# Attention and two MLPs on one core: the planner's order replaced by written tables, with filler products in PE's early waits

## The chip, the cores and the metric

The kernel runs on one core of a Trainium2 chip. The metric is the device time of one execution in microseconds (us). The core has TensorE (PE, with its weight loads as PEld), VectorE (DVE), ScalarE (ACT), GpSimd (POOL), and SyncE (SP), which issues nearly all DMAs.

## The reference

Three stages follow one another on 4 sequences of 576 positions: block-causal attention (8 heads of 64, blocks of 64 positions), an MLP with a gate from a three-tap convolution over positions, and an MLP whose second half is normalized and mixed over positions. All is float32.

```python
scores = scale * np.matmul(q, k.transpose(0, 1, 3, 2))
scores = np.where(block_i >= block_j, scores, -1000000000.0)
attn = np.exp(scores - np.max(scores, axis=-1, keepdims=True))
attn = attn / (np.sum(attn, axis=-1, keepdims=True) + 1e-09)
x = heads_side_by_side(np.matmul(attn, v))          # [4, 576, 512]
...
h = np.maximum(x @ w_in, 0.0)                       # moe: 512 -> 1024
x = (h / (1.0 + np.exp(-conv3(h, conv_w)))) @ w_out # 1024 -> 512
...
u, v = halves(np.maximum(x @ w2_in, 0.0))           # moe2: 2 x 512
v_n = (v - mean(v)) / np.sqrt(var(v) + 1e-06)
gated = u * (np.einsum('ts,bsd->btd', w_spatial, v_n) + b_spatial[None, :, None])
out = gated @ w2_out
```

## The kernel before, in words

Most products are made of three: each float32 operand is split into a rounded high part and the rest, and PE multiplies high by high, high by rest and rest by high. The splits are work for ACT (high part), DVE and POOL (the rest).

PE's work is cut into 429 steps of five streams, and each stream keeps its own order. The attention goes through 16 pairs of heads, p = 0 to 15.

- **x** (80 steps, five for each pair, x5p to x5p+4): four products `max_step` (L566) whose row maxima DVE reduces, and one transpose `max_tr` (L643) of the maxima. x4 is the transpose of pair 0, x9 that of pair 1, x24 that of pair 4. Between the fourth and the fifth stands DVE's `max_up`. After the transpose ACT or DVE copies the result to `mt`, and a DMA spreads it as a row of `mq`; x3, x5, x10 and so on may take both banks of the ring `mo` in place of one of `st`.
- **s** (66 steps, `score`, L731): scores of a pair, for which the row of maxima must have come; ACT takes the exponential and so frees the slot. For pair 0, s0 and s1 are the first part, without the row, and s2 and s3 add the row to the same slots.
- **v** (16 steps, `av`, L753): probabilities by values; `v_out` and `s_out` copy the result and the sums out, and `norm_a` (L825) sends the sums through three DMAs and multiplies.
- **m** (129 steps, `in1` L857 and `out1` L900): the first MLP. `out1` stores its result to DRAM through a buffer `y`.
- **p** (138 steps, L1135 to L1298): the second MLP, after the attention is over; it begins in the last steps of m.

Around PE run tasks: `prep_pair` (L496) loads a pair's keys and queries and makes kp and qp (its tasks `one` and `ends`; for pairs that are not multiplied in plain float32 it also subtracts the rest), `split64` (L446) loads and splits 64K weights, `load_vs` loads values, `add_up` adds exponentials, `combine` and `store` finish the output.

The order of everything is made when the program is built. Class `Order` (L104) keeps a clock with a cost for each step and task (functions `t_act`, `t_dve` and so on) and at each moment gives each engine the ready task of the best priority, in `kick` (L185), and PE a step, by `pick_at` (L1001), which weighs how far the m stream lags behind the attention against constants such as `AHEAD` and `TILE_ON`. Buffer slots are given out first free, first taken (`grab`, L224). The engines then run their instructions in the order of that emission; each waits on semaphores for what it needs.

PSUM has the ring `st` (three slots of two banks) and `mo` (two banks). Sixteen products of 256 columns on a set tile (`spin`, L1037) run on PE before the first data are there; they write to the last slot of `st`. SP issues, in order: pair 0's two parts, `ident`, the first `v`, `cwr`, pairs 1 and 2, then weights.

Of the kernel before, what the change touches and what calls it, by code (L numbers as in the profile page):

```python
# [16 lines left out]
NP = H // 2  # L17
# [12 lines left out]
AHEAD = (0.05, 2.01, -0.09, 0.71)  # L30
# [30 lines left out]
EARLY_M = 3  # L61
TILE_ON = 0.55
JOIN = 0.3
S_FIRST = 3
HOLD = 0
STKEEP = 2
MARGIN = 0
STICK = 0
# [11 lines left out]
XE = (0.95, 13.95)  # L80
XMO = 11
XK = 0.35
WR = 2
SPIN = 16
SLACK = 0.8
# [17 lines left out]

class Order:  # L104
# [9 lines left out]
    def __init__(self, rings):  # L114
        self.t = 0.0
        self.heap = []
        self.seq = 0
        self.done = set()
        self.waiting = {}
        self.free = dict(rings)  # L120
# [5 lines left out]
        self.flying = 0  # L126
        self.pick = None
        self.cost = 0.0
        self.tile = False
        self.port = 0.0  # L130
        self.when = {}
        self.extra = {}
        self.times = {r: [-9.0] * n for r, n in rings.items()}
        self.slots = {r: [None] * n for r, n in rings.items()}
# [5 lines left out]
    def spawn(self, gen, group="x", lag=0.0):  # L140
        self.live[group] = self.live.get(group, 0) + 1
        self.push(self.t + lag, lambda: self.advance(gen, group))

    def advance(self, gen, group, got=None):
        while True:
# [11 lines left out]
            elif kind == "take":  # L157
                n = it[2] if len(it) > 2 else 1
                if self.free[it[1]] >= n and not any(r[0] == it[1] for r in self.ring_wait):
                    got = self.grab(it[1], n)  # L160
# [15 lines left out]
    def enqueue(self, it, gen, group):  # L176
        eng, dur, fn = it[:3]
        lat = (it[3] if len(it) > 3 else 0.0) + (0.03 if eng == "ACT" else 0.0)
        prio = it[4] if len(it) > 4 else 1
        port = it[5] if len(it) > 5 else False  # L180
        self.seq += 1
        heapq.heappush(self.ready.setdefault(eng, []), (prio, self.seq, dur, fn, lat, gen, group, port))
# [20 lines left out]
    def mark(self, key):  # L203
        self.done.add(key)
        self.when[key] = self.t
# [3 lines left out]
    def release(self, ring, slots):  # L209
        self.free[ring] += len(slots)  # L210
        self.times[ring] += [self.t] * len(slots)
        self.slots[ring] += slots
        for r in list(self.ring_wait):
            if r[0] == ring:
                if self.free[ring] < r[1]:
                    break
                got = self.grab(ring, r[1])
                self.ring_wait.remove(r)
                self.push(self.t, lambda r=r, got=got: self.advance(r[2], r[3], got[0] if r[1] == 1 else got))
# [4 lines left out]
    def grab(self, ring, n):  # L224
        self.free[ring] -= n
        del self.times[ring][:n]
        got = self.slots[ring][:n]
        del self.slots[ring][:n]
        return got

    def reset(self, ring, slots):
        self.free[ring] = len(slots)
        self.times[ring] = [self.t] * len(slots)
        self.slots[ring] = list(slots)

    def can(self, step, margin=0.0):
        if "alts" in step:
            for ring, keep in step["alts"]:
                step["ring"], step["rings"] = ring, step["base"] + [(ring, 1)]
                if self.free[ring] > keep + self.extra.get(ring, 0) and self.fits(step, margin):  # L240
                    return True
            return False
        return self.fits(step, margin)

    def fits(self, step, margin):
        return all(k in self.done and self.when[k] <= self.t - margin for k in step["needs"]) and all(
            self.free[r] >= n and self.times[r][n - 1] <= self.t - margin
            for r, n in step["rings"])

    def pe(self):  # L250
# [5 lines left out]
        got = {r: self.grab(r, n) for r, n in step["rings"]}  # L256
# [7 lines left out]
        def end():  # L264
# [5 lines left out]
            for gen, group in after or ():  # L270
                self.spawn(gen, group, self.PE_HOP)
# [13 lines left out]
def dma(size, fn, prio=0, issue=0.48):  # L285
    yield ("SP", issue, fn, 0, prio)
    yield ("sleep", 0.5)
# [21 lines left out]
def attn_moe_moe2_kernel(  # L309
# [104 lines left out]
    ALTS = [("mo", 0), ("st", 0)]  # L414

    mk = att.tile([128, S], F32R, name="mk")
# [29 lines left out]
    def split64(src, hi, lo, key, prio=None):  # L446
        prio = P_W if prio is None else prio
        unit = {"w1i": 0, "w1o": 8, "w2i": 16, "w2o": 24}[key[0]] + key[-1] + (4 * key[1] if len(key) > 2 else 0)
        yield ("take", "wr")
        home = "wn" if key[0] != "w2i" and (od.free["wn"] or od.free["x1"] <= X1KEEP[key[0] == "w1o"]) else "x1"  # L450
# [4 lines left out]
        yield from dma(524288, lambda: nc.sync.dma_start(  # L455
# [4 lines left out]
        yield ("free", "wr")  # L460
# [20 lines left out]
    def load_pairs():  # L481
        for p in range(NPAIR):
            if not f32_scores(p):
                yield ("take", "late")
# [3 lines left out]
            od.spawn(prep_pair(p, RAW[p], slot), "att")  # L488
# [3 lines left out]
    def first_load(o, i, part):  # L492
        yield from dma(o.shape[1] * o.shape[2] * 512, lambda: nc.sync.dma_start(out=o, in_=i), -1)
        yield ("mark", ("raw", 0, part))

    def prep_pair(p, t, slot):  # L496
# [4 lines left out]
        if p:  # L501
            yield from dma(2 * S * 4 * 128, lambda: nc.sync.dma_start(out=t, in_=src), P_RAW)
# [19 lines left out]
        for i, c in enumerate(parts):  # L522
# [3 lines left out]
            od.spawn(one(act(kp[:, c], t[:, 0, c], n), ("kpq", p, i, 0)), "att")  # L526
            od.spawn(one(second(qp[:, c], t[:, 1, c], n), ("kpq", p, i, 1)), "att")
# [6 lines left out]
        od.spawn(ends(), "att")  # L534
# [11 lines left out]
        yield ("free", "late")  # L546
# [3 lines left out]
    def load_vs():  # L550
        yield ("sleep", 0.06)
        for p in range(NPAIR):
# [3 lines left out]
            yield from dma(327680, lambda: nc.sync.dma_start(out=t, in_=vt[b, g]), P_V)  # L556
# [968 lines left out]
```

## Time and profile before

| | us |
|---|---|
| median of 3 runs | 614.19 (613.38 to 614.73) |
| profiled execution | 615.53 |
| its span, first to last instruction | 613.8 |
| PE busy | 582.1 (95%) |
| DVE busy | 458.7 (75%) |
| ACT busy | 252.8 (41%) |
| POOL busy | 220.3 (36%) |

The profiled execution's time is the span and 1.7 us around it. PE's matmuls are pipelined and their ends are modelled. The granted clock is the share of 2.4 GHz that PE was given; it has two levels, 1.2 and 2.4 GHz. Idle time of an engine counts only where it holds up the engine that sets the end. A line such as L342 is that of a helper (`mm`) through which most products go.

### The profile page before, as it was taken

The page shows a single profiled execution, that of the slowest core. Times are in us where ns is not written, and L with a number is a line of the kernel's source. Part 1 is how long each engine was busy: PE and PEld are TensorE (multiplying, and loading weights), DVE is VectorE, ACT ScalarE, POOL GpSimd, SP SyncE. Part 2 cuts the span into 40 slices and gives each one's busy share as a digit, 9 for nine tenths or more (in the row PEclk, how much of TensorE's full clock was granted, in tenths as well). Part 3 has the DMA queues.
Part 4 walks back from the last instruction along what each step waited for, and adds up shares of the span by engine and source line. Part 5 has one row for each costly group of instructions (what it writes and reads, how often), then busy time and mean ns, then how long its engine had stood idle before and what let it go on. Part 6 is the DMA issues. An engine that isn't in the chain of part 4 may idle for free.

```text
span 613.8 us, 11943 instructions
## 1 busy us (share of the span) xinstructions
PE 582.1 (95%) x4596; PEld 519.1 (85%) x4596; DVE 458.7 (75%) x930; ACT 252.8 (41%) x517; POOL 220.3 (36%) x269
## 2 busy tenths in 40 slices
PE   6888879989999999999999999999999999999997
PEld 4556657969897788779988998999989999998996
DVE  4898899986929986985936399986697576368256
ACT  3465555644345632435626174636153023013101
POOL 5321343565352647435525253642212112022020
PEclk7698989999999999999999999999999999999999
DMA  7364543024031233212020374434713300610002
GB/s 238 109 206 150 183 160 141 1 90 129 30 129 42 67 115 120 81 60 82 1 78 21 105 250 132 153 105 116 237 36 106 127 19 1 194 40 2 28 31 79
DMA packets 43543, 61.23 MB, mean 100 GB/s; under 512 B 8949, under 2 KB 34293, under 8 KB 43486
## 3 DMA queue, kind: packets, MB, share of 16 engines
q1 hardware_dynamic: 43226, 60.37, 30.3%
q8 instruction: 36, 0.59, 0.4%
q14 instruction: 21, 0.17, 0.1%
q0 software_dynamic: 256, 0.09, 0.1%
q10 hardware_dynamic: 4, 0.00, 0.0%
HBM read 46.08 MB, written 14.23 MB: 98 GB/s over the span
## 4 chain that ended last, share of the span: by engine, by line
PE 56%; DVE 27%; DMA 5%; ACT 4%; issue 3%; POOL 2%; SPq 1%; ACTq 0%; DVEq 0%; POOLq 0%
PE mo L342 33%; PE s L342 9%; DVE cc L882 5%; PE st L350 4%; PE st L712 4%; DVE cc L886 3%; DVE mx L592 3%; PE st L704 2%; DMA w_raw<-in_w2o_dram 2%; DMA raw<-in_kq_dram 2%; PE st L716 2%; DVE g L356 2%; DVE w_f L443 2%; PE st L587 1%; DVE w_raw L441 1%
## 5 line engine op out<-in xcount | busy, mean ns | idle before, releaser
L342 PE MATMUL mo<-x,w1i_h 128*128 128x290 f32 x504 | 109.1, 303 | 1.7 <-DVE y L919 1.2
L342 PE MATMUL mo<-g,w1o_h 128*128 128x288 f32 x464 | 98.3, 298 | 0.8 <-ACT h L876 0.4
L882 DVE SCALAR_TENSOR_TENSOR cc<-h,cwt,cc 128x288 f32<-128x288 f32 x128 | 77.8, 623 | 18.1 <-ACT cc L879 17.5
L342 PEld LDWEIGHTS mo<-x,w1i_h 128*128 128x128 f32 x504 | 83.5, 189 | 5.7 <-issue 2.3
L342 PEld LDWEIGHTS mo<-g,w1o_h 128*128 128x128 f32 x464 | 76.2, 189 | 3.2 <-issue 1.5
L342 PE MATMUL mo<-x,w1i_l 128*128 128x290 f32 x252 | 75.3, 299 | 0.0
L342 PE MATMUL mo<-g,w1o_l 128*128 128x288 f32 x232 | 68.5, 295 | 0.0
L353 POOL TENSOR_SCALAR g<-cc 128x288 fp32r<-128x288 f32 x64 | 40.1, 632 | 77.7 <-DVE cc L886 69.7
L725 ACT ACTIVATE e<-st 128x640 f32<-128x640 f32 (+1 forms) x64 | 52.5, 836 | 31.1 <-PE st L716 30.4
L353 POOL TENSOR_SCALAR g<-ga 128x288 fp32r<-128x288 f32 x40 | 19.0, 474 | 108.3 <-DVE ga L1225 73.4
L342 PE MATMUL mo<-x,w2i_h 128*128 128x288 f32 x256 | 52.4, 296 | 0.5 <-ACT u L1199 0.3
L342 PEld LDWEIGHTS mo<-x,w1i_l 128*128 128x128 f32 x252 | 47.8, 190 | 0.0
L350 PE MATMUL st<-e,v 128*64 128x448 f32 (+4 forms) x384 | 47.2, 395 | 0.4 <-ACT e L725 0.3
L592 DVE TENSOR_REDUCE mx<-st 128x2 f32<-128x128 f32 (+3 forms) x64 | 42.3, 684 | 4.9 <-PE st L587 3.4
L350 PEld LDWEIGHTS st<-e,v 128*64 128x64 f32 x384 | 25.3, 138 | 23.2 <-issue 17.0
L342 PEld LDWEIGHTS mo<-g,w1o_l 128*128 128x128 f32 x232 | 43.6, 188 | 0.1
L342 PEld LDWEIGHTS mo<-x,w2i_h 128*128 128x128 f32 x256 | 41.4, 188 | 1.5 <-ACT u L1199 1.2
L716 PE MATMUL st<-mq,mk 64*128 64x320 f32 (+1 forms) x192 | 39.4, 406 | 1.2 <-DMA mq<-mt 1.2
L879 ACT ACTIVATE cc<-h,cwt 128x288 f32<-128x288 f32 x64 | 34.3, 536 | 12.9 <-DVE g L356 6.9
L342 PE MATMUL s<-w2i_h,x 128*128 128x512 f32 x128 | 39.5, 390 | 0.0
L342 PE MATMUL mo<-ws_h,vnh 128*128 128x288 f32 x135 | 39.4, 296 | 0.0
L884 ACT ACTIVATE cc<-cc 128x288 f32<-128x288 f32 x64 | 28.1, 440 | 27.1 <-DVE cc L882 26.6
(184 smaller groups left out, 1432.1 us busy)
## 6 DMA issues: line engine op xcount, KB each, us to landing
x2d<-y SPq DMA_DIRECT2D x32, 288.0 KB
x<-x2d SPq DMA_DIRECT2D x16, 576.0 KB
raw<-in_kq_dram SPq DMA_DIRECT2D x15, 576.0 KB
v<-in_vt_dram SPq DMA_DIRECT2D x16, 320.0 KB
rb<-rd SPq DMA_DIRECT2D x32, 144.0 KB
out_dram<-o SPq DMA_DIRECT2D x32, 144.0 KB
x<-in_w2i_dram SPq DMA_DIRECT2D x8, 512.0 KB
w_raw<-in_w1i_dram SPq DMA_DIRECT2D x4, 512.0 KB
```

Of the source, the lines that this page charges most:

```text
L342: nc.tensor.matmul(o, w, x, start=start, stop=stop)
L350: nc.tensor.matmul(o[row:row + m], w, x, start=start, stop=stop)
L353: nc.gpsimd.tensor_scalar(o, i, 1.0, 0.0, ALU.mult, ALU.add)
L356: nc.vector.tensor_tensor(o, a, b, ALU.subtract)
L592: return ("DVE", t_dve(2 * i.shape[-1] * (i.shape[2] if len(i.shape) == 4 else 1)), lambda: nc.vector.tensor_reduce(o, i, AX.X, ALU.max), ...
L712: nc.tensor.matmul(st[:, e, o:o + nq], keys(kx, slice(64 * e, 64 * e + 64)), qx[e], start=j == 0, stop=False)
L716: nc.tensor.matmul(st[:, e, o:o + nq], keys(mk, r), q[r, q0:q0 + nq], start=False, stop=True)
L725: yield ("ACT", t_act(2 * n), lambda: nc.scalar.activation(ex[:, :, e0:e0 + n], st[:, :, 0:n], ACTF.Exp, scale=0.125), 0, 0)
L879: yield ("ACT", t_act(HT, False, 1), lambda: nc.scalar.activation(cc, h[:, o:o + HT], ACTF.Copy, scale=cwt[:, c, 1:2]), 0, P_G)
L882: yield ("DVE", t_dve(HT, ptr=1), lambda: nc.vector.scalar_tensor_tensor(cc, h[:, o + e:o + e + HT], cwt[:, c, j:j + 1], cc, ALU.mult, ALU ...
L884: yield ("ACT", t_act(HT, False), lambda: nc.scalar.activation(cc, cc, ACTF.Tanh, scale=0.5), 0, P_G)
L886: yield ("DVE", t_dve(HT), lambda: nc.vector.scalar_tensor_tensor(cc, cc, 1.0, h[:, o:o + HT], ALU.add, ALU.mult), 0, P_G, True)
```

## The change

The planner's choice is taken out. `SEQ` names the stream of each of PE's steps in turn: x, y (an x step in the ring `mo`), s, v, m, p (a capital takes `st` in place of `mo`), and f, a filler. `ORDER` names, for DVE, ACT, POOL and SP, the task whose next instruction comes next, and `BIND` names which slot each task takes in every ring. `Order` keeps its clock, but an engine waits for the named task where before it took any ready one. `HOME` says which weight blocks lie in which buffer. `HOT` is 0, so that the new wait in `dma` does nothing.

Beside the order, four things are new: a tile `full` of 222 columns; the opening products run on it with 222 columns and write columns 290 to 511 of the first bank of `mo`; a filler is two rounds (`FILL_N`), in the tiled mode two products a round, one on each half of the rows, one to each bank of `mo`; and the steps x4, x9, ... and the m steps name `ident` and `cwt` as needs. All other instructions are those of before.

Set beside the order that the planner emits, the tables keep PE's steps but for 52 of 429, which stand at most three places elsewhere; DVE has 638 of 919 entries elsewhere, by 1.5 places on average over all and 21 at most, ACT 270 of 515 (at most 11), POOL 93 of 254 (at most 9) and SP 139 of 209 (at most 11). In the opening PE had `x3 s1 x4 x5 x6 s2 x7 s3 x8 s4` and has `x3 x4 x5 x6 f s1 f s2 s3 f x7 x8 s4`. The fourth filler stands between x31 and x32. SP had `first_load0 first_load1 later load_vs start2 prep_pair11 prep_pair22` (`later` is ident, `start2` is cwr). ACT had `one100 one101 one200 one201 ends2 x4 ends2 x4` (the second x4 is a DMA issue), `split64.5 one400 ends4 v1 v1.2`, and `s28 s29 s30 s31 split64.15 split64.16 one900 v6`. DVE had `norm_a1 split64.8 norm_a1 x24 x25 x26`, `add_up9 x58 m38 add_up9 m38 add_up9 max_up11` and `split64.3*3 m114`. PE had `x59` between m40 and m41.

```diff
-AHEAD = (0.05, 2.01, -0.09, 0.71)
...
-TILE_ON = 0.55
-JOIN = 0.3
...
+FILL_N = 2
+HOT = 0.0
+SEQ = (
+    "xsxxyxyxfsfssfxxssxyxxvsxsssxyxxvxssssxyxxvsxsssxyxfxvsxssxyxsxmvsxmmmxxmxxxmmmmmmmmmsssssvxxmxxxmms"
...
+ORDER = {
+    "DVE": (
+        "one001 x0*2 one011 x0 x1 x2 x1 x2 x3*3 max_up0 x5*2 x6*2 split64 x6 split64 x5 split64 x7*2 x8*2 max_up1 "
+        "split64.2 start2 split64.2 x9 start2 x11 x10 x11 split64.3 x12 start2 split64.3 x10 split64.3 x12 x10 x11 v0 "
...
+        "x20 split64.8 max_up4 split64.8 x24 x25 norm_a1 x27 x25 x26 norm_a1 norm_a2 split64.9 norm_a1 x26 x27 "
...
+    "ACT": (
+        "one000 one010 one101 ends2*2 one100 x4 start2 x4 one201 one200 split64 split64.2 s2 s3 split64 s4 s5 split64.3 "
+        "one300 split64.2 split64.3 ends3*2 s6 split64.4 s7 split64.5 s8 s9 split64.4 split64.6 split64.5 v1.2 v1 ends4 "
+        "s10 ends4 s11 one400 split64.7 s12 s13 split64.6 split64.8 split64.7 v2 s14 one500 s15 one501 s16 s17 "
...
+    "SP": (
+        "first_load0 first_load1 first prep_pair22 prep_pair11 load_vs later start2 split64 split64.2 x4 load_vs "
...
+BIND = {
...
+    "st": (
+        "x0:0 s0:1 x1:2 x2:0 x4:0 x6:0 s1:2 x7:0 x8:1 s4:2 s5:0 x9:2 x11:1 x12:0 v0:2 s6:0 x13:1 s7:2 s8:0 s9:2 x14:1 "
...
     def kick(self, eng):
-        if self.busy.get(eng) or not self.ready.get(eng):
+        if self.busy.get(eng):
             return
-        _, _, dur, fn, lat, gen, group, port = heapq.heappop(self.ready[eng])
+        key = ""
+        if eng in self.order:
+            if self.at[eng] == len(self.order[eng]):
+                return
+            key = self.order[eng][self.at[eng]]
+        if not self.ready.get((eng, key)):
+            return
+        dur, fn, lat, gen, group, port = self.ready[eng, key].pop(0)
+        self.at[eng] = self.at.get(eng, 0) + 1
...
+    def open(self, ring, name, n):
+        if (ring, name) not in self.bind:
+            return len(self.free[ring]) >= n
+        k = len(self.bound.get((ring, name), ""))
+        return all(i in self.free[ring] and self.line[ring, i][0] == name for i in self.bind[ring, name][k:k + n])
...
+    full = att.tile([128, 222], F32R, name="full")
...
     def pick():
-        if stay():
+        if pos["at"] == len(SEQ):
             return None
-        return (pick_at(MARGIN) if pos["m"] >= EARLY_M else None) or pick_at(0.0)
+        c = SEQ[pos["at"]]
+        step = head(c)
+        if step is None:
+            return None
...
+        if not od.can(step):
             return None
+        pos["at"] += 1
...
     def spin(o):
 
-        x = w1i_l[:, 0, 0:256]
-        nc.vector.memset(raw(x), 1.0)
+        nc.vector.memset(raw(full), 1.0)
         for _ in range(SPIN):
-            nc.tensor.matmul(o[:, 0, 0:256], x[:, 0:128], x, start=True, stop=True)
+            nc.tensor.matmul(o[:, 290:512], full[:, 0:128], full, start=True, stop=True)
+
+    def fill(got):
+        o = od_mo[0]
+        for _ in range(FILL_N):
+            if od.tile:
+                for e in range(2):
+                    r = slice(64 * e, 64 * e + 64)
+                    nc.tensor.matmul(od_mo[e][:, 290:512], full[r, 0:128], full[r], start=True, stop=True)
+                od.cost += 0.113
+            else:
+                mm(o[:, 290:512], full[:, 0:128], full, True, True)
 
     def start2():
-        spin(od.slots["st"][-1])
+        spin(od_mo[0])
```

## Rows read from the trace of the kernel before

**Rows 1.** The page, part 1: busy us (share of the span) xinstructions, by engine.
```profile
PE 582.1 (95%) x4596; PEld 519.1 (85%) x4596; DVE 458.7 (75%) x930; ACT 252.8 (41%) x517; POOL 220.3 (36%) x269
```

**Rows 2.** Stretches: busy us (instructions) of PE, PEld, DVE, ACT, POOL; PEclk; DMA; GB/s.
```profile
9.50:26.00 16.50, 11.66 (x50) 7.40 (x52) 11.37 (x27) 8.21 (x16) 3.29 (x4) 0.50 0.37 122
26.00:57.00 31.00, 26.14 (x316) 17.74 (x316) 28.26 (x61) 17.23 (x31) 9.12 (x9) 1.00 0.59 193
57.00:63.50 6.50, 6.50 (x47) 5.87 (x49) 4.23 (x10) 4.21 (x7) 0.00 (x0) 0.50 0.31 101
63.50:87.50 24.00, 18.89 (x226) 13.03 (x224) 22.45 (x44) 12.79 (x23) 10.41 (x9) 1.00 0.48 168
87.50:95.50 8.00, 7.50 (x43) 5.97 (x45) 7.92 (x16) 4.77 (x9) 3.12 (x4) 0.57 0.54 201
95.50:120.00 24.50, 24.50 (x212) 22.09 (x208) 24.31 (x49) 15.38 (x36) 10.12 (x12) 1.00 0.19 70
120.00:460.00 340.00, 331.91 (x2649) 298.18 (x2648) 263.42 (x494) 159.09 (x325) 151.84 (x171) 1.00 0.31 98
```

**Rows 3.** Timeline of PE, opening: start, duration, what, idle before and releaser.
```profile
1.20 3.79 PE L1042 MATMUL st<-w1i_l 128*128 128x256 f32 x16 [1.20 <-DVE eps L1046]
...
10.16 1.23 PE L704 MATMUL st<-raw 64*128 64x256 f32 x4
11.71 0.38 PE L647 MATMUL st<-ident,mx 128*9 128x128 f32 x1 [0.33 <-DVE mx L640]
...
14.22 0.80 PE L587 MATMUL st<-kp,qp 64*128 64x128 f32 x4 [1.59 <-ACT mt L652]
16.26 0.72 PE L716 MATMUL st<-mq,mk 64*128 64x320 f32 x2 [1.25 <-DMA mq<-mt]
18.40 0.69 PE L587 MATMUL st<-kp,qp 64*128 64x384 f32 x2 [1.41 <-DVE mxu L592]
...
19.99 1.87 PE L704 MATMUL st<-raw 64*128 64x448 f32 x4 [0.27 <-ACT e L725]
```

**Rows 4.** Timeline of ACT, opening.
```profile
10.77 0.68 ACT L510 ACTIVATE kp<-raw 128x576 fp32r<-128x576 f32 x1 [4.86 <-DMA raw<-in_kq_dram]
...
12.61 0.68 ACT L510 ACTIVATE kp<-raw 128x576 fp32r<-128x576 f32 x1 [0.59 <-DMA raw<-in_kq_dram]
...
13.92 0.25 ACT L652 ACTIVATE mt<-st 9x128 fp32r<-9x128 f32 x1
```

**Rows 5.** Timeline of the DMA issues on SP, opening.
```profile
2.10 0.60 SPq L1068 DMA_DIRECT2D ident<-in_cst_dram  x1
...
3.69 0.91 SPq L502 DMA_DIRECT2D raw<-in_kq_dram  x2
```

**Rows 6.** Timelines of ACT (first row) and PE, 42 to 57 us.
```profile
42.54 0.67 ACT L510 ACTIVATE kp<-raw 128x576 fp32r<-128x576 f32 x1
...
44.23 0.70 PE L704 MATMUL st<-raw 64*128 64x256 f32 x4 [0.95 <-ACT srow L817]
...
56.95 0.58 PE L712 MATMUL st<-qp,kp 64*128 64x256 f32 x2 [2.45 <-ACT xp L805]
```

**Rows 7.** Timeline of DVE, 48 to 63 us.
```profile
48.35 1.65 DVE L356 TENSOR_TENSOR raw<-raw,kp 128x576 fp32r<-128x576 f32 x1
...
59.34 0.33 DVE L844 TENSOR_TENSOR xp<-xp,rb 128x160 f32<-128x160 f32 x1
...
60.19 0.45 DVE L844 TENSOR_TENSOR xp<-xp,rb 128x288 f32<-128x288 f32 x1
62.73 0.28 DVE L654 CAST mt<-st 9x128 fp32r<-9x128 f32 x1 [2.09 <-PE st L647]
```

**Rows 8.** Timeline of PE at three waits after 120 us.
```profile
133.46 0.53 PE L342 MATMUL st<-kp,qlast 128*128 128x288 f32 x2 [1.81 <-ACT mt L652]
...
200.87 0.28 PE L647 MATMUL st<-ident,mx 128*9 128x128 f32 x1 [1.27 <-DVE mx L640]
...
381.20 0.40 PE L342 MATMUL mo<-x,w1i_h 128*128 128x290 f32 x1 [0.87 <-DVE y L919]
```

More of the change, by code (lines that the diff above doesn't have):

```diff
@@ L101, in words, with expand, unpack @@
     return w.bitcast(U32).rearrange("r (f t) -> r f t", t=2)
+def expand(text):
+    out = []
+    for word in text.split():
+        name, _, n = word.partition("*")
+        out += [name] * int(n or 1)
+    return out
+def unpack(table):
+    seq, line = {}, {}
+    for ring in table:
+        for word in table[ring].split():
+            name, _, ids = word.partition(":")
+            for i in ids:
+                i = int(i, 36)
+                seq.setdefault((ring, name), []).append(i)
+                line.setdefault((ring, i), []).append(name)
+    return seq, line
 class Order:
@@ L126, in __init__ @@
         self.flying = 0
+        self.hot = 0.0
+        self.names = {}
+        self.count = {}
+        self.order = {e: expand(ORDER[e]) for e in ORDER}
+        self.at = {e: 0 for e in ORDER}
         self.pick = None
@@ L130, in __init__ @@
         self.port = 0.0
[L131 to L134, printed above, removed]
+        self.slots = {}
+        self.free = {}
+        self.used = {}
+        self.bound = {}
+        self.bind, self.line = unpack(BIND)
+        for r, n in rings.items():
+            self.reset(r, [None] * n)
     def push(self, t, fn):
@@ L158, in advance @@
                 n = it[2] if len(it) > 2 else 1
-                if self.free[it[1]] >= n and not any(r[0] == it[1] for r in self.ring_wait):
-                    got = self.grab(it[1], n)
+                if self.open(it[1], self.names[gen], n):
+                    got = self.grab(it[1], self.names[gen], n)
                     got = got[0] if n == 1 else got
@@ L221, in over, with grab @@
     def over(self, group):
         return self.flying == 0 and self.live.get(group, 0) == 0
[L224 to L229, printed above, removed]
+    def grab(self, ring, name, n):
+        k = self.bound.get((ring, name), [])
+        ids = self.free[ring][:n] if (ring, name) not in self.bind else self.bind[ring, name][len(k):len(k) + n]
+        self.bound[ring, name] = k + ids
+        for i in ids:
+            self.free[ring].remove(i)
+            if (ring, i) in self.line:
+                self.line[ring, i].pop(0)
+        self.used[ring] += ids
+        return [self.slots[ring][i] for i in ids]
@@ L245, in fits, with can @@
[L245 to L248, printed above, removed]
+        self.free[ring] = list(range(len(slots)))
+        self.used[ring] = []
+    def can(self, step):
+        return all(k in self.done for k in step["needs"]) and all(self.open(r, step["name"], n) for r, n in step["rings"])
     def pe(self):
@@ L255, in pe @@
             return
-        got = {r: self.grab(r, n) for r, n in step["rings"]}
+        got = {r: self.grab(r, step["name"], n) for r, n in step["rings"]}
         tile = step.get("tile", False)
@@ L282, in run, with dma @@
             fn()
-def dma(size, fn, prio=0, issue=0.48):
+def dma(od, size, fn, prio=0, issue=0.48, hot=False):
+    if size > 65536:
+        while od.t < od.hot:
+            yield ("sleep", 0.1)
     yield ("SP", issue, fn, 0, prio)
+    if hot:
+        od.hot = 0.0
     yield ("sleep", 0.5)
@@ L487, in load_pairs @@
             HELD[p] = [slot]
-            od.spawn(prep_pair(p, RAW[p], slot), "att")
+            od.spawn(prep_pair(p, RAW[p], slot, late), "att")
             if p == 0:
@@ L954, in attn_moe_moe2_kernel @@
-    mw = [sum(st["w"] for bb, st in mstream if bb == b) for b in range(B)]
-    pos = dict(s=0, v=0, x=0, m=0, da=0.0, dm=0.0)
+            mstream.append(out1(b, hf, m, part))
+    pos = dict(s=0, v=0, x=0, m=0, p=0, at=0)
     nx = 5
-    def take(k, stream):
-        pos[k] += 1
-        if pos["v"] > NP:
-            pos["da"] = (pos["s"] / 2 + 2 * pos["v"]) / (4 * NP) - 1.0
-        return stream[pos[k] - 1]
-    def ready(k, stream, margin):
-        return pos[k] < len(stream) and od.can(stream[pos[k]], margin)
```

367 lines of the change are left out of this document (209 added, 158 removed), and 159 rows, old and new, of tables (BIND, ORDER).

## The prediction

> **What bounds the kernel now.** I read the page first, then the busy time by stretches, then PE's timeline where it waits, and last the queues of ACT, SP and DVE at those places. PE is busy 582.1 of 613.8 us, so 31.7 us without PE work are all that a new order can win by shortening waits [rows 1]. The stretches say where they lie: PE stands idle 4.8 us between 9.5 and 26, 4.9 up to 57, 5.1 between 63.5 and 87.5, and 8.1 in the long stretch from 120 to 460 [rows 2]. A second loss hides inside the busy time. In three stretches the granted clock is 0.50, 0.50 and 0.57, the lower level of 1.2 GHz, and elsewhere 1.00, that is 2.4 GHz [rows 2]. Work that PE does there takes twice its time: half of 11.66, half of 6.5 and about half of 6.9 us (8 us at 0.57 are 6.9 at the lower level), 12.5 us in all. The last thing to see is DVE: 28.26 of 31.0 us from 26 on, 22.45 of 24.0 from 63.5 and 24.31 of 24.5 from 95.5 are busy, so up to 120 us it is nearly as full as PE, and what PE wins early it must find again in DVE's idle time, 5.1 us of it between 9.5 and 26 [rows 2].
>
> **What moves.** PE's 429 steps keep their order but for 52 that stand at most three places elsewhere. The waits must therefore change through the other queues, and there the moves are many but short (counts in the section on the change). I price the places where a row shows PE waiting and the tables move the releaser or what stood ahead of it, take the rest at nothing, and keep that rest as a source of error.
>
> **The opening.** PE's three waits of 1.59, 1.25 and 1.41 us (x6, s2, x7) hang on one event [rows 3]. The transpose x4 is done at 12.09, but ACT copies it only at 13.92, because pair 2's kp and qp (from 12.61) stand ahead of it [rows 3, 4]. x6 needs the slot that this copy frees, and s2 needs the row that the copy sends. The table puts pair 1's q copy, both ends2 and pair 1's k copy ahead of x4's copy, and pair 2's two behind it: 0.68 for each of the two, about 0.25 for each end, 1.85 us of ACT from the moment that pair 1 lands [rows 4].
>
> When does it land? Before, it was issued at 3.69 and ACT started on it at 10.77; pair 2, next in the queue, came at 12.61, 1.84 us later for 576 KB, 320 KB a us [rows 4, 5]. SP's table issues both pairs ahead of ident, v and cwr, so pair 1's issue comes about 1.2 us sooner (near 2.5), but pair 2 is ahead of it. If only the issue counted, it would land at 9.6; if only the bytes ahead counted, 576 KB more and 408 KB fewer, 0.5 us later, 11.3. I take 10.5, near the middle, since the issue and the bytes both have rows: x4's copy starts at 12.35, 1.55 us sooner (bounds 0.8 and 1.8, the latter set by x4 itself).
> The Trainium skill, DMA: Bandwidth & Descriptors, section Queues, rings and completion order, says that on each DMA engine descriptors are taken in ring order. The 1.84 us between the two pairs agrees. By that rule alone the landing is 11.3, the copy comes 0.8 us sooner instead of 1.55, and the sum below would end 0.75 higher, at 609.4.
>
> x6 then starts at 12.65 and takes 0.8 (13.45). Now the new pieces: a filler, s1 (which used to run at 10.16 inside the wait for x4 and so cost nothing; now its 1.23 us lie on PE's path), and a second filler [rows 3]. A filler here is four products of 222 columns on the two row halves, two at a time; the sixteen opening products of 256 columns took 3.79 us, 0.237 each, so 0.205 for 222, and 0.41 for a filler [rows 3]. s2 can start at 15.5, the row being there by 14.7. Then s2 0.7, s3 0.4, a third filler 0.4: x7 at 17.0, since the table has x6's last reduction ahead of the 1.06 us weight step it used to stand behind. x7 and x8 take 1.3, s4 starts at 18.3 against 19.99: 1.7 us won. The three fillers are 1.2 us that I count on the path.
>
> The clock adds to it. It rose at 26, when PE had had its last long wait, which ended at 18.40, behind it [rows 2, 3]. In the new order the last long wait ends at 12.65, 5.75 sooner; if the rise moves by as much, it comes at 20.3. From s4 on, 6.5 us of work at the lower level remained (19.99 to 26.5); 2.0 of them pass before 20.3, and 4.5 take 2.25: another 2.25 us won, with bounds 0 (the clock rises when it did) and 3.25 (it is up by 18.3). The sum for PE is 3.95. DVE can follow: it had 5.1 us idle here, and its weight steps of slice 2 now stand behind max_up1; I let it keep 0.45 more. **Opening: 3.5 us won, bounds 0.5 and 4.7** (copy 0.8 sooner and no help of the clock; copy 1.8 sooner and 3.25 from the clock; each less the 0.45). The opening products themselves, now 222 columns and not 256, end some 0.4 us sooner, but x3 then waits for POOL's qlast as before, so this counts nothing.
>
> **26 to 120 us.** At 44.23 PE waits 0.95 for v1's copies, with one400's 0.67 us ahead of them in ACT's queue; the table puts one400 behind: 0.6 won [rows 6]. Against that, DVE now takes x24's copy ahead of norm_a1's products, while before it filled the time up to a 2.09 us idle stretch with two of them, 0.33 and 0.45 [rows 7]; if that idle stretch is still there, DVE has 0.8 us more to do behind it. Up to 0.8 lost, 0 if the clock is up by then; I take 0.3. The fourth filler, at the upper level and before x32, costs 0.2. **0.1 won, bounds 0.4 lost and 0.6 won.**
>
> **After 120 us** PE is the bound (331.91 of 340), so a wait that goes is time won. x59 waited 1.27 us for max_up11, which stood behind four steps of add_up9; it now stands ahead of them, and x59 two steps later in PE: 1.27 won. m116 waited 0.87 for m114's evacuation, which now passes one weight step of 0.69: 0.7 won. [rows 8]. Both are counted in full, because nothing but PE's own work follows them there. **2.0 us won**; bounds 0, if the moved steps open waits of the same size, and 5, if the other waits of this stretch shrink alike. Past 460 the order of PE is unchanged, the stores of the last batch keep their places but for two swaps, and I count nothing.
>
> **Sum.** 3.5 + 0.1 + 2.0 = 5.6 us. The rows are from an execution of 615.53 us with a span of 613.8, and 1.3 us above the median of the runs, 614.19; the difference is taken from the median, since it does not hang on that 1.3: **608.6 us**.
>
> **The rivals.** *The clock stays up* (0.20). The second fall of the clock came with PE's wait of 2.45 us before 56.95, the third near 87.5 after waits of its own; waits of 1.81 and 1.27 us at 133.46 and 200.87 left it at 1.00 [rows 2, 6, 8]. If the opening's lead and the moved steps keep these waits that short, 3.25 us (half of 6.5) and 3.4 us (half of 6.9) come back: one of them gives 605.2 to 605.4, both 602.0. For it: the first of these waits follows v2's copies, ahead of which DVE spent 1.65 us on prep_pair30's subtraction [rows 7], and the half of that step that runs on POOL moves away from beside it. Against it: norm_a0, which v2 needs, keeps its place in DVE.
>
> *DVE swallows it* (0.14). If DVE, nearly full up to 120, keeps all of its idle time but 1 us, and the waits after 120 only change places, 1 us is left: 613.2, between 612 and 615.4. For it: PE's early waits end on DVE or on ACT steps that wait for DVE. Against it: DVE's 5.1 idle us in the opening lie just where the tables act.
>
> *Slower: a step at the head of a queue that is not ready* (0.16). Where before DVE did whatever was ready by its planner's clock, the table may name a step that is late on the chip, and everything behind waits. The place is DVE between 26 and 120: at x24 the price is the 0.8 us above. There are about eight such pairs in that stretch; at 0.8 to 1.2 each, 6.4 to 9.6 us, the sum is 615.0 to 618.2, and with the opening at its low bound 618.0 to 621.2. It decides when DVE's idle time from 26 to 120, now 6.8 us [rows 2], grows by 6.8 to 13.6, for then the sum passes 615.4.
> The Trainium skill says of it, in PSUM — Partial Sum Buffer, section Engine vs sequencer instructions, that the queues of ScalarE and VectorE are strict FIFO. DVE's 2.09 us before 62.73 [rows 7] do not contradict it, though they do not show that a ready step stood behind; by this rule the moves that put waiting steps first cost their full wait, and the time would be this rival's.
>
> **Chances.** The forecast has 0.50, between 606 and 611; the clock 0.20 (602 to 606); no gain 0.14; slower 0.16. The range 602 to 615.4 leaves out nearly all of the slower case. The likeliest case alone: 606 to 611. Within 0.2%, 1.2 us, is about what a measurement of this kernel tells from no change: 0.04 of the no-gain case lies below 613, so faster 0.74, same 0.10, slower 0.16.
>
> **What will show it.** Right: ACT's copy for x4 before 12.8, s4 before 18.8, granted clock at 1.00 before 22, x59 and m116 without a wait, and PE busy near 581 us: 2.25 less at the lower level, 1.4 more for the fillers. Wrong: pair 1 landing after 12 (the opening is then lost), the clock still rising near 26, DVE idle between 26 and 120 above 8 us, or new PE waits between 120 and 460 that bring its idle time back to 8. Most doubtful is what I took at nothing: some 600 moved entries of DVE with no row of a PE wait behind them.

## The result, and the profile after

| | us |
|---|---|
| before, median of 4 runs | 613.79 (610.94 to 614.73) |
| after, median of 4 runs | 606.76 (606.29 to 607.56) |
| ratio | 0.9895 (95%: 0.9859 to 0.9930) |
| profiled execution of after, its span | 607.56, 605.7 |

The change makes the kernel 1.05% faster (0.7 to 1.4%), 7.0 us between the medians; 5.6 were forecast. Part 1 of the page of after, which answers to [rows 1]:

```profile
PE 576.7 (95%) x4612; PEld 515.0 (85%) x4612; DVE 443.8 (73%) x930; ACT 249.1 (41%) x517; POOL 214.1 (35%) x269
```

PE is busy 5.4 us less, and DVE 14.9 us less on the same 930 instructions. The busy time by stretches, at the times of [rows 2] and with their columns:

```profile
9.50:26.00 16.50, 13.58 (x100) 9.57 (x104) 12.77 (x32) 10.08 (x18) 4.52 (x5) 0.74 0.63 197
26.00:57.00 31.00, 25.61 (x321) 18.28 (x314) 29.08 (x58) 18.82 (x31) 9.57 (x9) 1.00 0.50 159
57.00:63.50 6.50, 6.11 (x85) 4.04 (x83) 6.36 (x16) 3.09 (x5) 1.69 (x4) 1.00 0.73 257
63.50:87.50 24.00, 17.70 (x162) 11.59 (x164) 20.67 (x39) 11.54 (x21) 5.21 (x5) 0.86 0.41 135
87.50:95.50 8.00, 8.00 (x105) 5.89 (x101) 7.57 (x17) 4.21 (x8) 4.09 (x4) 1.00 0.57 209
95.50:120.00 24.50, 22.58 (x159) 20.81 (x158) 24.23 (x51) 15.55 (x38) 11.04 (x14) 1.00 0.16 57
120.00:460.00 340.00, 335.96 (x2693) 303.90 (x2692) 255.26 (x504) 158.87 (x335) 148.45 (x170) 1.00 0.31 97
```

In the opening the granted clock is 0.74 on average and no longer 0.50 throughout, and PE does 13.58 us of work there where it did 11.66. There is one more fall of the clock, between 72 and 80 (0.86 in its stretch), where before had two. From 120 to 460 PE is idle 4.0 us, where it was 8.1. From 26 to 120 DVE stays as full as it was (6.1 us idle, 6.8 before). PE's opening, beside [rows 3]:

```profile
9.48 0.85 PE L651 MATMUL mo<-kp,qlast 128*128 128x288 f32 x2 [2.24 <-POOL qlast L662]
11.93 0.37 PE L959 MATMUL st<-ident,mx 128*9 128x128 f32 x1 [1.60 <-DMA ident<-in_cst_dram]
12.57 0.82 PE L651 MATMUL mo<-kp,qlast 128*128 128x288 f32 x2 [0.27 <-ACT kp L821]
13.32 0.79 PE L898 MATMUL st<-kp,qp 64*128 64x128 f32 x4
13.91 0.60 PE L1330 MATMUL mo<-full 64*128 64x222 f32 x4
...
16.65 1.11 PE L898 MATMUL st<-kp,qp 64*128 64x384 f32 x4
17.57 1.20 PE L1016 MATMUL st<-raw 64*128 64x448 f32 x4
...
22.84 1.57 PE L659 MATMUL st<-e,v 128*64 128x128 f32 x10 [0.47 <-DVE mt L966]
```

13.91 is the first filler. x4, at 11.93, waits 1.60 us for `ident`, which SP now issues behind pairs 1 and 2; before, it started at 11.71. x6 starts at 13.32 (14.22 before), x7 at 16.65 (18.40), s4 at 17.57 (19.99), and the first `av` at 22.84, 3.66 sooner than before. ACT, beside [rows 4]:

```profile
10.64 0.68 ACT L821 ACTIVATE qp<-raw 128x576 fp32r<-128x576 f32 x1 [5.19 <-DMA raw<-in_kq_dram]
...
12.34 0.27 ACT L964 ACTIVATE mt<-st 9x128 fp32r<-9x128 f32 x1
...
13.76 0.68 ACT L821 ACTIVATE qp<-raw 128x576 fp32r<-128x576 f32 x1 [1.04 <-issue]
```

ACT starts on pair 1 at 10.64, copies x4 at 12.34 where it was 13.92, and takes pair 2 (13.76) behind it. Five later places of PE, x29, the fourth filler and x32, then x59 and m116:

```profile
70.48 0.28 PE L959 MATMUL st<-ident,mx 128*9 128x128 f32 x1 [1.64 <-DVE mx L951]
...
73.46 0.77 PE L1330 MATMUL mo<-full 64*128 64x222 f32 x4 [2.02 <-DVE mxl L938]
74.02 0.56 PE L898 MATMUL st<-kp,qp 64*128 64x384 f32 x2
...
199.71 0.27 PE L959 MATMUL st<-ident,mx 128*9 128x128 f32 x1
...
374.54 0.30 PE L651 MATMUL mo<-x,w1i_h 128*128 128x290 f32 x1
```

x59 and m116 have no wait any more, where [rows 8] show 1.27 and 0.87. But the fourth filler waits 2.02 us itself, for x30's first reduction on DVE.

### The profile page after: what moved, and what is told of

Its sections match the earlier page's. It is cut to its first block, busy times and chain, and to the rows that moved or that the text cites. A ratio compares the mean times of both kernels' runs of the same rounds, so it can differ in the third digit from the quotient of the medians.

```text
span 605.7 us, 11928 instructions
## 1 busy us (share of the span) xinstructions
PE 576.7 (95%) x4612; PEld 515.0 (85%) x4612; DVE 443.8 (73%) x930; ACT 249.1 (41%) x517; POOL 214.1 (35%) x269
## 4 chain that ended last, share of the span: by engine, by line
PE 62%; DVE 12%; ACT 2%; issue 1%; POOL 1%; DVEq 0%; POOLq 0%; ACTq 0%
PE mo L651 41%; PE s L651 11%; PE st L659 3%; DVE cc L1195 3%; PE st L1024 3%; DVE cc L1199 1%; PE st L651 1%; DVE g L665 1%; DVE mx L903 1%; PE st L1028 1%; PE st L1016 1%; PE st L898 1%; DVE w_f L753 1%; DVE x L665 0%; DVE mxu L903 0%
## 5 line engine op out<-in xcount | busy, mean ns | idle before, releaser
L1195 DVE SCALAR_TENSOR_TENSOR cc<-h,cwt,cc 128x288 f32<-128x288 f32 x128 | 71.1, 573 | 21.0 <-ACT cc L1192 20.3
L1037 ACT ACTIVATE e<-st 128x1024 f32<-128x1024 f32 (+1 forms) x64 | 53.1, 836 | 32.3 <-PE st L1028 26.1
L659 PE MATMUL st<-e,v 128*64 128x448 f32 (+4 forms) x384 | 49.2, 407 | 0.5 <-DVE mt L966 0.5
L903 DVE TENSOR_REDUCE mx<-st 128x2 f32<-128x640 f32 (+2 forms) x64 | 42.5, 679 | 6.1 <-PE st L898 5.8
L651 PE MATMUL mo<-x,w2i_l 128*128 128x288 f32 x128 | 37.7, 294 | 0.0
```

Source lines behind the costliest of these rows:

```text
L651: nc.tensor.matmul(o, w, x, start=start, stop=stop)
L659: nc.tensor.matmul(o[row:row + m], w, x, start=start, stop=stop)
L903: return ("DVE", t_dve(2 * i.shape[-1] * (i.shape[2] if len(i.shape) == 4 else 1)), lambda: nc.vector.tensor_reduce(o, i, AX.X, ALU.max), ...
L1037: yield ("ACT", t_act(2 * n), lambda: nc.scalar.activation(ex[:, :, e0:e0 + n], st[:, :, 0:n], ACTF.Exp, scale=0.125), 0, 0)
L1195: yield ("DVE", t_dve(HT, ptr=1), lambda: nc.vector.scalar_tensor_tensor(cc, h[:, o + e:o + e + HT], cwt[:, c, j:j + 1], cc, ALU.mult, ALU ...
```

## The experiments

The planner's order can be written out as tables too (with the new opening products on `full`), and wherever both orders have done the same set of entries, one can be cut and joined to the other. So stretches and single engines can be exchanged. Ratios are to the kernel before, run in the same job; the lead of one trace over another is the difference of the starts of the same PE step.

**The change in three stretches.** Order, slots and PE's sequence are the tables' in one stretch and the planner's elsewhere.

```diff
 DVE, ACT, POOL, SP entries and PE steps that are the tables'
-none (planner's order)
+open_only: the first 45, 24, 9, 18 and 21 (fillers 1 to 3 with them)
+mid_only:  from there to 247, 137, 51, 64 and 105 (filler 4)
+late_only: from there to the end
```

> The planner's order of before, but with the tables' order of every queue, their slots and the first three fillers up to about 27 us. If the prediction's term for the opening holds (3.5 us won; the profile of after shows v0 3.7 us sooner), v0 starts near 22.8 and the time is 3.5 to 3.7 us under that of before. If DVE, nearly full up to 120, swallows what PE wins early, v0 still starts near 22.8 but x39 near 100 is no sooner than before, and the time is within 1 us of before.

Measured: 610.11 us, ratio 0.9947 (0.9926 to 0.9968), so 3.25 us won (2.0 to 4.5). v0 starts at 23.23, and x39 at 98.04 where it was 103.21: DVE does not swallow it.

> The planner's order, but with the tables' order from about 27 to 122 us alone, the fourth filler with it. By the prediction's term this is worth 0.1 us (0.4 lost to 0.6 won). By the profile of after, whose lead shrinks from 3.7 us at v0 to some 2.5 us near 120, it loses about 1 us. The rival, that the middle needs the opening's lead to come out right, gives more than 2 us lost.

Measured: 613.85 us, ratio 1.0008 (0.9990 to 1.0025): 0.5 us lost, between 1.5 lost and 0.6 won. Not more than a loss of the size that the trace of after shows.

> The planner's order up to about 122 us, the tables' order from there to the end. By the prediction's terms (x59 and m116 alone) 2.0 us are won. By the profile of after, whose lead grows from some 2.5 us near 120 to 7.4 at the end, 4.9 us. If the gain there came only from what the early part handed on, under 1 us.

Measured: 608.88 us, ratio 0.9929 (0.9903 to 0.9955): 4.35 us won (2.8 to 5.9). The gain of this stretch is its own. The three ratios multiply to 0.9884, the whole change has 0.9895: the parts add up. No run has the planner's order as tables with nothing of the change in it; since all three runs hold that form and their product still meets the whole, it can't be worth much by itself.

**The fillers.** Left out of `SEQ`, the fourth by itself and the first three by themselves.

```diff
 after
-    "xsxxyxyxfsfssfxxssxyxxvsxsssxyxxvxssssxyxxvsxsssxyxxvsxsssxyxfxv ...
 no_fill4
+    "xsxxyxyxfsfssfxxssxyxxvsxsssxyxxvxssssxyxxvsxsssxyxxvsxsssxyxxv ...
 no_fill123
+    "xsxxyxyxsssxxssxyxxvsxsssxyxxvxssssxyxxvsxsssxyxxvsxsssxyxfxv ...
```

> The changed kernel without its fourth filler, the one between x31 and x32. The prediction priced that filler at 0.2 us. In the profile of after it does not fill a wait, it waits itself: 2.02 us for the reduction of x30, whose bank of mo it writes, and x32 and v4 stand behind it. By this theory x32 starts up to 2 us sooner, TensorE's clock does not fall before v4 (v4 then takes 4.5 us and not 6.9), and the time is 2 to 4.5 us under that of after. Rival: x32 waits for its own slot as long, or v4 for its own data, and the time is within 0.5 us of after.

Measured: 606.58 us, ratio 0.9888 (0.9866 to 0.9911), no different from after (0.9895). PE's timeline without it, x31 with x32 behind it in one group, v4, and x34:

```profile
70.27 0.72 PE L905 MATMUL st<-kp,qp 64*128 64x128 f32 x6
70.92 1.57 PE L666 MATMUL st<-e,v 128*64 128x128 f32 x10
...
83.10 0.28 PE L966 MATMUL st<-ident,mx 128*9 128x128 f32 x1 [2.50 <-DVE mx L958]
```

The first half of the theory holds: x32 starts at 70.61, 3.4 us sooner than the 74.02 of after, and v4 at 70.92, 3.6 sooner. The second half holds only in part: x34 now waits 2.50 us for DVE, and v5 is only 1.8 sooner. DVE is busy for 23.0 of the 24 us from 63.5 on (20.7 in after), and half of what PE wins is handed back at DVE's next result. The rest is still there at the end of this trace (its span is 603.6, that of after 605.7), but this execution was the shortest of its five, and the medians do not show it.

> The changed kernel without the three fillers of the opening (x6 to x7); the fourth stays. By the prediction's account they lie on PE's path, 0.41 us each at the lower clock, and give nothing back: the time is 0.5 to 1.4 us under that of after. Rival, the fillers are what lets the clock rise near 18: without them PE is idle in their place, the clock rises later than 22, v0 comes at 24 or later where it came at 22.84, and the time is 1 to 2.5 us above that of after. If both are small, PE waits for pair 1's second reductions anyhow, x7 starts at the same time, and the time is within 0.5 us.

Measured: 608.44 us, ratio 0.9944 (0.9923 to 0.9964). That is above after (0.9895, and 0.9905 when run again), though the intervals still touch. The trace shows both theories at work. Without the fillers s4 starts at 17.18, 0.39 sooner: they do lie on PE's path, at a third of the price in the forecast, since x7 waits 0.65 us for x6's last reduction in their place. But v0 starts at 23.52, 0.68 later. The stretches of this run, then of after, with PEclk third from the end:

```profile
16.00:18.00 2.00, 1.73 (x9) 1.12 (x10) 1.94 (x5) 0.98 (x3) 1.58 (x1) 0.50 0.00 0
18.00:20.00 2.00, 2.00 (x14) 1.55 (x12) 1.96 (x3) 0.82 (x2) 1.27 (x1) 0.50 0.47 145
20.00:22.00 2.00, 2.00 (x14) 1.33 (x12) 1.92 (x6) 0.80 (x1) 0.00 (x0) 0.50 0.33 117
22.00:24.00 2.00, 1.91 (x17) 1.29 (x17) 1.46 (x6) 1.58 (x2) 0.00 (x0) 0.94 0.44 76
```

```profile
16.00:18.00 2.00, 2.00 (x14) 1.54 (x12) 1.94 (x5) 1.34 (x3) 1.58 (x1) 0.50 0.01 3
18.00:20.00 2.00, 1.77 (x18) 1.16 (x14) 1.93 (x4) 1.37 (x2) 1.03 (x1) 0.97 0.29 91
20.00:22.00 2.00, 1.65 (x19) 1.22 (x17) 1.92 (x6) 1.43 (x3) 0.24 (x1) 1.00 0.70 199
```

The clock is back at 1.00 at 18 with the fillers and at 22 without. From s4 to v0 PE takes 6.34 us here and 5.27 in after. The loss does not last in this trace: by x39 it is 1.2 us ahead of after's, since its clock falls for 3.4 us in the middle and not for 6.8, and the two spans end level (605.6 and 605.7). The two longest of its six executions, 610.25 and 611.06 us, have a mean granted clock of 0.975; the other four, at 607.45 to 608.95, have 0.982 to 0.997.

**The order of GpSimd alone**, put back to the planner's: 93 entries of 254, of which these are around 200 us.

```diff
 POOL
-m37 m39*2 m38 norm_a8 m40 prep_pair110 m38 m40
+m37 m38*2 m39*2 norm_a8 m40 norm_a8 m40 prep_pair110
...
```

> The changed kernel with the planner's order of GpSimd alone (93 of 254 entries stand elsewhere). In the profiles DVE spends 15 us less on the same instructions after the change (505.7 to 489.8 us in sum), because fewer of its steps stand blocked while GpSimd runs one. If the order of GpSimd is what avoids that, the sum goes back above 497 and the time rises by 1 to 4 us over after. If the order of DVE avoids it, the sum stays under 493 and the time within 1 us of after. A third way: GpSimd's head step comes late, and the time rises by more than 4 us through waits on it.

Measured: 613.77 us, ratio 1.0021 (1.0008 to 1.0035): all that was won is gone. The same kernel was run once more for its profile.

> The changed kernel with the planner's order of GpSimd again, for a profile that can be set against that of after. It took 613.8 us, so all that was won is lost. If blocked DVE steps cost it, DVE's sum of busy time is above 497 us and the loss is spread over many places. If a late head step of GpSimd costs it, the sum stays under 493 and PE has a few waits of 1 us and more that end on GpSimd or on DVE behind it, most of them between 170 and 250, where the order of GpSimd differs most.

Measured: 613.70 us. DVE's sum is 491.8, so blocked steps are not what it costs. Up to x59 this order is even 2.1 us ahead of after; then it loses 4.9 us at one step, s46. GpSimd there, and PE's s46, two of its products:

```profile
191.88 0.43 POOL L668 TENSOR_SCALAR g<-cc 128x288 fp32r<-128x288 f32 x1 [4.95 <-DVE cc L1205]
200.66 1.85 POOL L668 TENSOR_SCALAR g<-cc 128x288 fp32r<-128x288 f32 x1 [8.35 <-DVE cc L1205]
...
203.37 0.44 POOL L668 TENSOR_SCALAR g<-cc 128x288 fp32r<-128x288 f32 x1
...
208.03 2.24 POOL L675 TENSOR_TENSOR raw<-raw,qp 128x576 fp32r<-128x576 f32 x1
```

```profile
204.95 0.31 PE L1030 MATMUL st<-qp,raw 64*128 64x320 f32 x2
210.32 0.64 PE L1030 MATMUL st<-raw,kp 64*128 64x320 f32 x2 [5.06 <-POOL raw L675]
```

GpSimd stands idle for 8.35 us before 200.66, because the entry at its head is m38, whose product DVE finishes at 200.51. m39's was finished at 197.51 and had to stand behind; `prep_pair110`'s subtraction, behind all of them, ends at 210.27, and s46 waits 5.06 us for it (0.48 in after). Behind this step about 3 us more go in smaller pieces, 1.3 of them at m44. The tables of DVE and GpSimd agree on m39 before m38; here DVE's is worth nothing without GpSimd's. The other way round was not run.

**Steps of DVE taken out from beside GpSimd.** In the trace of after, DVE's max_up5 and the step behind it, then GpSimd's two subtractions of `prep_pair50`, then the same two DVE steps in the trace of before:

```profile
69.02 1.41 DVE L951 TENSOR_TENSOR mx<-mx,mxu 64x8 f32<-64x8 f32 x1
70.45 1.86 DVE L665 TENSOR_TENSOR w1o_l<-w_f,w1o_h 128x512 fp32r<-128x512 f32 x1
```

```profile
69.00 1.40 POOL L669 TENSOR_TENSOR raw<-raw,kp 128x576 fp32r<-128x576 f32 x1 [5.12 <-PE st L1028]
70.36 1.41 POOL L669 TENSOR_TENSOR raw<-raw,qp 128x576 fp32r<-128x576 f32 x1
```

```profile
73.74 0.16 DVE L640 TENSOR_TENSOR mx<-mx,mxu 64x8 f32<-64x8 f32 x1
73.94 0.69 DVE L356 TENSOR_TENSOR w1o_l<-w_f,w1o_h 128x512 fp32r<-128x512 f32 x1
```

A step of 0.16 us took 1.41 and ended with GpSimd's instruction; one of 0.69 took 1.86. Pairing DVE's 930 instructions of the two traces by task and turn, 141 took over 0.15 us longer in one than in the other (85 in before, 56 in after), and all of these ran beside a GpSimd instruction, as about four in ten of DVE's do at all. Reductions from PSUM were never among them. The Trainium skill, SBUF — State Buffer, section Who interferes with whom, says that a DVE instruction with two SBUF inputs contends with a GpSimd instruction that reads SBUF, that the ports they share are an exclusive lock, and that `tensor_reduce` never contends on trn2; the rows agree.

```diff
 DVE (dodge; dodge_nofill4 is the same without the fourth filler)
-split64.4 x15 split64.5 x17 x16 x15 split64.6 x16 x18
+split64.4 x15*2 split64.5 x17 x16*2 split64.6 x18
-split64.7 norm_a0 x19
+split64.7 x19 norm_a0
-x28 split64.10 max_up5 split64.9 split64.10 x30 norm_a2 norm_a3 x31 x32 x31 x32 x30 x31
+x28 max_up5 split64.10 x30 x31 x32 x31 x32 x30 x31 split64.9 split64.10 norm_a2 norm_a3
```

> The changed kernel with three short moves in DVE's order that take steps out from beside GpSimd's subtractions: x15's last step and x16's last reduction ahead of split64.5 and split64.6, x19's copy ahead of norm_a0's product, and max_up5 and the reductions of x30 to x32 ahead of split64.10 and split64.9. In the profile of after these stand blocked for 1.05, 1.23, 1.25 and 1.17 us, and PE waits 1.52 (x18), 1.28 (x22), 1.64 (x29) and 2.02 (the fourth filler) for them. If the blocking sets these waits, all four are under 0.5 us, and the time is 3 to 6 us under that of after. If DVE's full queue up to 120 swallows it, the waits come back at x34 or x39 and the time is within 1 us of after.

> The same three moves, and the fourth filler left out too. If that filler's wait was for x30's first reduction alone, which now comes early, leaving it out adds 0 to 0.4 us to what the moves win. If DVE swallows the moves, this is within 1 us of after as well.

Measured: 605.57 us, ratio 0.9885 (0.9869 to 0.9900), and 604.45 us, 0.9867 (0.9854 to 0.9881). Three of the four waits are gone (x18 0.25, x29 and the filler none) and v4 starts at 69.51, 5 us sooner than in after. x22 still waits 1.27, because `split64.7`, still ahead of x19's copy, is now the one that is blocked. And x34, which did not wait in after, waits 1.53 for max_up6: of the 5 us at v4, 2.9 are left at v5. Against after_again (0.9905, below) dodge alone is no clear gain, where 3 to 6 us were expected. Leaving the fourth filler out as well gives 1.1 us more by the medians, and the intervals overlap.

```diff
 DVE (dodge6, on dodge_nofill4)
-norm_a0 norm_a1 split64.7 x19 norm_a0
+norm_a0 x19 norm_a1 split64.7 norm_a0
-x33 norm_a2 x33 split64.12 max_up6
+x33*2 max_up6 norm_a2 split64.12
 POOL
-split64.16 ends9*2
+ends9*2 split64.16
```

> The changed kernel once more, beside the next two on the same chip, so that they can be set against it. Expected: a ratio of 0.988 to 0.991 to before (606 to 608 us).

> The three moves in DVE's order without the fourth filler, and three more: x19's copy ahead of split64.7 too (in the run before, x22 still waited 1.27 us, because split64.7 stood blocked ahead of that copy), x33's second reduction and max_up6 ahead of norm_a2 and split64.12 (x34 waited 1.53 us for max_up6), and on GpSimd ends9 ahead of split64.16 (x45 waited 1.46 us for it). If the chip only needs these heads in time, the three waits fall under 0.4 us each, and the time is 2.5 to 4.5 us under that of the three moves alone, near 600 to 602 us. If DVE's full queue up to 120 is the bound whatever stands at its head, x34 and x39 take the waits back and the time is within 1 us of it.

Measured: after 607.51 us, 0.9905 (0.9879 to 0.9932); the six moves 604.03 us, 0.9846 (0.9816 to 0.9875). x22 and x34 wait no more, x45 0.57. But s23, which waits 0.57 in after, waits 1.99 for an exponential on ScalarE, as it already did behind the first three moves (1.96 in dodge); and the clock falls behind it. By the ratios 1.3 us are won over dodge_nofill4, where 2.5 to 4.5 were expected, and these intervals overlap too; against after_again the six moves and the missing filler together win 0.6%, and there the intervals do not.

```diff
 ACT (dodge8, on dodge6)
-split64.12 s22 s23
+s22 split64.12 s23
 DVE
-split64.11 norm_a2 split64.11 norm_a2 split64.12 split64.11 x30 x33*2 max_up6 norm_a2 split64.12
+split64.11 norm_a2 split64.11 norm_a2 x30 x33*2 max_up6 split64.12 split64.11 norm_a2 split64.12
```

> The six moves, and two more at the last place where PE waits long before TensorE's clock falls: on ScalarE s22's exponential ahead of split64.12's copy (s23 waited 1.99 us for it), and on DVE x30's last step, x33's reductions and max_up6 ahead of split64.12 and of split64.11's second part. If that wait is what the clock's fall near 78 follows, the clock stays at 1.00 there, v5 comes 4 to 5 us sooner than at 86.3, and the time is 3 to 5 us under that of the six moves (604.0). If the clock falls on the shorter waits that are left, only the 1.4 us of s23 are won. If DVE's queue takes it back at x36 or x39, the time is within 0.5 us of the six moves.

Measured: 602.59 us, ratio 0.9837 (0.9808 to 0.9866). PE at s23, s24 and x34 in dodge6 and its stretch, then s23, x34 and x36 in dodge8 and the same stretch:

```profile
76.60 0.39 PE L1031 MATMUL st<-qp,kp 64*128 64x256 f32 x2 [1.99 <-ACT e L1044]
...
78.03 0.47 PE L1031 MATMUL st<-qp,kp 64*128 64x448 f32 x2 [0.69 <-ACT e L1044]
...
80.23 0.39 PE L966 MATMUL st<-ident,mx 128*9 128x128 f32 x1
```

```profile
63.50:87.50 24.00, 20.11 (x187) 15.03 (x189) 21.41 (x48) 14.71 (x26) 7.76 (x7) 0.86 0.56 192
```

```profile
74.90 0.39 PE L1031 MATMUL st<-qp,kp 64*128 64x256 f32 x2 [0.56 <-ACT e L1044]
...
78.16 0.28 PE L966 MATMUL st<-ident,mx 128*9 128x128 f32 x1 [0.39 <-DVE mx L958]
...
80.95 0.60 PE L905 MATMUL st<-kp,qp 64*128 64x128 f32 x4 [1.95 <-DVE qp L831]
```

```profile
63.50:87.50 24.00, 20.05 (x191) 14.39 (x193) 21.62 (x48) 14.68 (x26) 8.11 (x7) 0.93 0.57 191
```

s23's wait is down from 1.99 to 0.56, and the clock stays up until 81; there x36 waits 1.95 for DVE's `one701`, and it falls, for 4 us where it was 7. v5 comes 0.8 sooner, not 4 to 5. The next head of a queue had taken over: by the ratios 0.6 us is won over dodge6, where 3 to 5 were expected, and the intervals overlap. This version has the lowest time of those run, 602.59 against 612.84 of before in its job, and its interval lies under that of after_again (0.9879 to 0.9932).

## Why the prediction came out right, and where its steps were off

The time (606.76 for 608.6) lies in the range and in the likeliest case. The signs named for it came: ACT's copy before 12.8, s4 before 18.8, the clock at 1.00 before 22, x59 and m116 without a wait. PE's busy time went further than the 581 said, to 576.7: the opening's work at the lower clock is shorter by more than was counted, and one of the middle's two falls is gone. By terms:

| term | forecast, us | alone, timed | lead in the trace of after |
|---|---|---|---|
| opening | 3.5 won (0.5 to 4.7) | 3.25 won | 3.66 at v0 |
| 26 to 120 | 0.1 won (-0.4 to 0.6) | 0.5 lost | 1.4 lost, v0 to m13 |
| after 120 | 2.0 won (0 to 5) | 4.35 won | 5.1 won, m13 to the last step |

**The opening** was right in size and half right in its parts. Of the two measures the 3.25 us of the timed runs is the better one: the lead of 3.66 is against a single, late trace of before, and mid_only and late_only, which have the planner's order there too, reach v0 at 25.05 and 25.54, only 2.2 and 2.7 us behind after. ACT's copy came at 12.34 (forecast 12.35), and that it came so close is partly luck. ACT started on pair 1 at 10.64, near the 10.5 taken between the two bounds; in the ten traces that hold this opening the start lies between 10.17 and 11.04. But x4 itself, done at 12.09 in the forecast, was done at 12.30, because it waited 1.60 us for `ident` (1.19 to 2.11 in the ten traces). The prediction names the move of `ident` behind the pairs and has no term for it. In after it seems to have cost nothing, since ACT was busy with pair 1's k copy until about the same time; in open_only and dodge ACT waits 0.31 and 0.33 us for x4. The Trainium skill, DMA: Bandwidth & Descriptors, section Queues, rings and completion order, says that on each DMA engine descriptors are taken in ring order. The 11.3 that the prediction got from this rule alone is later than any of the ten starts. s4 came at 17.57, 0.7 sooner than the sum had it, because the three fillers, counted at 1.2 us, mostly ran in a wait that was there anyway and cost 0.39. The clock's part was too large: 2.25 us were counted between s4 and v0. From s4 to v0 before took 6.51 at 0.50; two executions with the planner's opening took 6.00 with the clock back at 22 (mid_only) and 5.74 with no fall at all (late_only); after took 5.27, and after_again 5.38 with no fall at all. By these traces all of the clock is worth about 0.8 us there. DVE takes its place: in after PE waits 1.05 us for it between s4 and v0, in before not at all. That the fillers bring the clock back sooner was not foreseen. In seven of the nine traces that hold the three of them it is back between 16 and 19.2, and in two it does not fall; in the four without them it is back at 22 (no_fill123, mid_only) or 26 (before), or does not fall (late_only). What this is worth stays open: 0.68 us at v0 by the trace of no_fill123 and 2.4 to 3.0 by its ratio, with intervals that touch.

**The middle.** The fourth filler, priced at 0.2, waited 2.02 to 3.15 us for x30's first reduction in the five profiles that hold it with DVE's table as it was. Yet its removal brought no gain that the runs can tell, and half of the lead it gave at v4 was gone at v5, behind x34's wait for DVE: what the rival "DVE swallows it" said of the whole change is true, and in part, of this stretch alone. Its sign in the sum was wrong, within the noise of its own run. DVE's idle time from 26 to 120 is 6.1 us (6.8 before): it has not grown, and the slower rival is refuted for the change as made. Its mechanism is real: pool_undone shows a head step that is late, at 5 us for a single place, and on GpSimd, not DVE. The Trainium skill, PSUM — Partial Sum Buffer, section Engine vs sequencer instructions, says that the queues of ScalarE, VectorE and GpSimd are strict FIFO; the 8.35 us of GpSimd behind m38, of which m39 was ready for the last 3, agree.

**After 120** the step that was mis-sized is "x59 and m116, and the rest at nothing". Both came out as said, 1.43 and 1.03 us of lead at these steps. But x73, s56, x75, m108, p27, p10 and x57 bring 0.76, 0.62, 0.32, 0.54, 0.43, 0.26 and 0.27 more, 3.2 us together; s46, s61, p30 and the last steps take back 0.58, 0.85, 0.22 and 0.59. The other 1.7 of the 5.1 are x45 (0.42), v7 (0.25) and small changes, nearly all under 0.2. The prediction took all of these at nothing, having no row for what moved ahead of them; PE's idle time of 8.1 us in this stretch fell to 4.0, and as the bound of 5 said, most of it could go. Why each shrank was read from the traces alone: x73's releaser, x72's last reduction, had stood behind a product of m56 that took 1.08 us beside GpSimd; now it stands ahead. s56 had stood behind a product of norm_a10 of 1.56 us, now 0.91.

**The clock rival** got a part of its way: one fall in the middle instead of two. Only the two traces with the planner's order all the way to 120, before and late_only, have two falls behind 26; the other eleven, open_only and mid_only among them, have one. That fits the rival's condition, a lead from the opening or moved steps that keep waits short, but no run changes the clock alone, so the cause is not shown. Its price was too high. The prediction took half a microsecond for each one that PE works at the lower level. Over the 63 executions of before in the four jobs, time set against time at the lower level (worked out as twice the span times what the granted clock lacks to 1.00) gives a slope of 0.16 us for each one, an estimate with a correlation of 0.69. The clock alone does not explain the gain either: the median granted clock of late_only is that of before (0.977 and 0.978), and mid_only, with 0.9855, wins nothing.

DVE's 14.9 us less of busy time were in no term. They come with the late stretch (sums of DVE's durations: before 505.7, open_only 505.3, mid_only 507.1, late_only 489.1, after 489.8). How much of the 4.35 us they carry was not separated: the only run that took the gain away, pool_undone, left that sum at 491.8.

## What to carry to other kernels

Read an order as sets of heads that must agree: putting one engine's table back to the planner's cost all that the change had won, and a single late head cost 5 us of it. Where another engine is nearly full, a wait that is taken away can come back, in whole or in part, at the next result of that engine; follow the chain until a wait is gone for good before counting it. Look also at what a move puts back: `ident`, issued later, had a wait of its own that no term held. A filler is free only if it needs no slot that something else still holds.

## What the runs showed of the hardware that was not expected

The same order of instructions has its clock fall in different places from one execution to the next: with the planner's opening PE ran at 0.50 until 26, until 22, or not at all (before, mid_only, late_only), and after_again was never below 1.00 between 9 and 26, where after was until 18. A fall that one trace shows is a poor basis for a term of its own.

A DVE step of 0.16 us can take 1.41 beside one GpSimd subtraction, and the steps behind it wait with it; the durations of small DVE steps from one trace hold for another only where GpSimd stands as it did.
